# An attention and SwiGLU kernel: transposing x with VectorE and sixteen transfers instead of TensorE

## The chip, the core and the metric

The kernel runs on one core of one Trainium2 chip. The core has five engines that run their own instruction queues, each in order: TensorE (PE, matrix products into PSUM), VectorE (DVE), ScalarE (ACT), GpSimd (POOL) and SyncE (SP), which here only issues transfers. Transfers are carried by 16 DMA engines. The metric is the device time of one execution in microseconds, the median of several executions. A profiled execution, whose trace is read in this document, has its own span, which is a little shorter than the timed number.

## The reference

Two operations in sequence, all in float32:

```python
kv  = einsum('bhsd,bhse->bhde', k, v)          # per batch and head, 64 x 64
out = einsum('bhsd,bhde->bhse', q, kv)
x   = out / sqrt(mean(out*out, -1) + 1e-6) * g_norm
x   = x.transpose(0, 2, 1, 3).reshape(4608, 512)
y   = (silu(x @ w_gate) * (x @ w_val)) @ w_out  # 512 -> 1536 -> 512
```

There are 8 batches, 8 heads, 576 positions and head dimension 64, so x has 8 x 576 = 4608 rows of 8 x 64 = 512 columns. The root mean square is taken over each head's 64 values, so it is done per row and head. The weights arrive as 64-bit words and are rounded to float32 in the kernel.

## The kernel before, in words

**Blocks.** The 4608 rows are cut into nine blocks of 512 rows (four tiles of 128). One block holds rows of one or two batches. For every block the kernel has an *up stage* (x times w_gate and w_val, silu, product: h of 1536 x 512) and a *down stage* (h times w_out). Attention for block n+1 is worked in between: k^T v during the up stage of block n, q k^T v, the norm and the transposition during the down stage of block n. The class `Att` holds attention, `Ffn` the two stages.

**Matrix products.** They are done by a Strassen-Winograd scheme: seven products (numbered 1 to 7) of half-sized operands instead of eight, with sums of operands made beforehand on VectorE and GpSimd and sums of results made on VectorE. From block 2 on (`DEEP = 2`), the up stage does this at two levels (class `Inner`); the operand sums on the weight side were put into DRAM once and are streamed back as tiles `t` (L698). The sums on the x side are made by `sums` (L378): four of the first level in the tile `x`, which has seven parts of which 0 to 3 are x itself, then four of the second level, partly in the tile `xi`. The up stage's products are at L617. The down stage (class `Down`, products at L468) is one level deep; its products come in the order 1, 5, 6, 7, 2, 4, 3, here called P1, P5 and so on. Each is 24 matmuls of 128x128 by 128x256, as the profile counts them. P1, P6, P7 and P4 add onto one PSUM tile from the pool b and ScalarE copies out its state in between; P2 uses a; P5 and P3 use c. P5, P7 and P4 need operand differences `t` made by GpSimd (`turn_t`, L753).

**Attention in the down stage.** `steps` (L421) gives three pieces of work that `down` (L881) places behind P1, P6 and P2:

- behind P1, the first half (two of four row tiles): `product` (L312; q k^T v, 64 matmuls of 64x64, results in one PSUM tile of pool m and one of a; squares on ScalarE; sums of squares on VectorE, L338), `root` (L340; 1/sqrt by an integer first guess and three Newton steps on VectorE, 11 small instructions), `scale` (L358; x times the root, from PSUM into the tile `xts`);
- behind P6, `turn_x(0)` (L365): TensorE transposes the first half, eight 128x128 blocks through an identity matrix into PSUM pool m (L373), ScalarE copies them out with the gain g_norm (L374); then the second half of attention, its results in pools m and b;
- behind P2, `turn_x(1)`, then `sums`.

x has to be transposed because TensorE contracts over partitions: attention leaves rows on partitions, the up stage needs columns there.

**q, transposed already otherwise.** From block 3 on (`TURNED = 3`) q is not transposed by TensorE: `load_quarters` (L235) loads it in pieces of 32 columns, so that each 32x32 block lands where its transpose belongs, and VectorE transposes every 32x32 block in place of its own (L300). These are 32 transfers, or 16 for the last block, with rows of 128 bytes (L247); `down` issues them behind P5 for the block after the next.

**What sets the order.** The code emits instructions in the order that the loops give; the tile framework then orders every engine's queue by its own estimate of when things are ready, and sets semaphores for the dependencies between engines. Since a queue runs in order, an instruction that waits also holds what stands behind it on its engine. Tiles come from pools with a fixed number of buffers (`ring()`, five buffers of 128x2048, holds q transposed, the squares, `xts`, and the result sums; x has one buffer; PSUM pools a, b, c, m have 1, 3, 2 and 2 banks), and a new tile waits until the old one in its buffer is no longer read. Transfers also wait for the earlier one on the same of eight completion semaphores.

Of the kernel before, what the change touches and what calls it, by code (L numbers as in the profile page):

```python
# [8 lines left out]
F32 = mybir.dt.float32  # L9
# [3 lines left out]
ACT = mybir.ActivationFunctionType  # L13

P = 128
# [3 lines left out]
def kernel(  # L19
# [41 lines left out]
    nc = tc.nc  # L61
# [6 lines left out]
    HB = BLK // 2  # L68
    HD = DM // 2
    NB = NT // BLK  # L70
# [9 lines left out]
    def pool(name, bufs, **kw):  # L80
        return ctx.enter_context(tc.tile_pool(name=name, bufs=bufs, **kw))
# [4 lines left out]
    x_pool = pool("x", 1)  # L86
# [7 lines left out]
    a_psum = pool("a_psum", 1, space=PS)  # L94
    b_psum = pool("b_psum", 3, space=PS)
    c_psum = pool("c_psum", 2, space=PS)
    m_psum = pool("m_psum", 2, space=PS)
# [4 lines left out]
    gain = consts.tile([P, 1], F32, name="gain")  # L102
# [12 lines left out]
    def ring():  # L115

        return r_pool.tile([P, 4, BLK], F32, name="r")
# [67 lines left out]
    class Att:  # L185
# [126 lines left out]
        def product(self, i, pools=None):  # L312

            pools = pools or (m_psum, m_psum)
            self.ps[i] = [pool.tile([P, 2, NS, D], F32, name=pool.name[0]) for pool in pools]
            for t in range(2):  # L320
                for j in range(NS):
                    for b, _, p0, p1 in self.parts(2 * i + t):
                        for p in range(p0, p1, D):
                            for u in range(2):
                                rows = slice(u * D, (u + 1) * D)
                                nc.tensor.matmul(  # L326
                                    self.ps[i][u][p : p + D, t, j, :],
                                    lhsT=self.qt[rows, 2 * i + t, j, p : p + D], rhs=kvs[b % 3][rows, j, :],
                                    start=True, stop=True,
                                )  # L330
            if self.z is None or self.n:
                self.z = st_pool.tile([P, 2, 2, 2, NS], F32, name="z")
            if i == 0:
                self.sq = ring().rearrange("p f (t j d) -> p f t j d", t=2, j=NS)
            for u in range(2):
                sq = self.sq[:, 2 * i + u]
                nc.scalar.activation(out=sq, in_=self.ps[i][u], func=ACT.Square)  # L337
                nc.vector.tensor_reduce(out=self.z[:, i, u], in_=sq, axis=mybir.AxisListType.X, op=OP.add)  # L338
# [26 lines left out]
        def turn_x(self, i):  # L365
            if i == 0:
                self.x = x_pool.tile([P, 7, 2, HB], F32, name="x")
            xt = self.xts[:, i].rearrange("p t j u d -> p t j (u d)")
            for j in range(0, NS, 2):
                ps = m_psum.tile([P, 2, 2, P], F32, name="m")  # L370
                for e in range(2):
                    for t in range(2):
                        nc.tensor.transpose(ps[:, e, t], xt[:, t, j + e], ident)  # L373
                nc.scalar.activation(  # L374
                    out=self.x[:, 2 * i + j // 2], in_=ps.rearrange("p e t c -> p e (t c)"), func=ACT.Copy, scale=gain
                )

        def sums(self):  # L378

# [41 lines left out]
        def steps(self):  # L421


            def last():
                self.turn_x(1)
                if self.n:
                    self.sums()

            def middle():
                self.turn_x(0)  # L430
                self.half(1, (m_psum, b_psum))


            return [lambda: self.half(0, (m_psum, a_psum)), middle, last]

    CHAIN = {1: ("b", True), 6: ("b", False), 7: ("b", False), 4: ("b", False), 2: ("a", True),
             5: ("c", True), 3: ("c", False)}
# [5 lines left out]
    DEEP = 2  # L443

    TURNED = 3

    class Quad:


        def __init__(self, steps):  # L450
            self.steps = steps
            self.ps, self.room = {}, None

            self.apart = {}
# [94 lines left out]
    class Inner:  # L549
# [36 lines left out]
        def whole(self, g, o):  # L586

            return self.shared[g][:, o].rearrange("p f e q t -> p (f e) (q t)")
# [242 lines left out]
    class Ffn:  # L831
# [49 lines left out]
        def down(self, nxt):  # L881

            down = self.down_
            fill = dict(zip((1, 6, 2), nxt.steps() if nxt else ()))
            for p in (1, 5, 6, 7, 2, 4, 3):
                if p == 1:
                    down.turn_t(7, self.ended)
                if p == 6:
                    down.turn_t(4, nxt.halves[0] if nxt and nxt.n >= TURNED else None)
                down.multiply(p)  # L890
                self.make(12)
                if p == 5:
                    for i in range(2):
                        self.loads(i)
                if p in fill:
                    fill[p]()
                if p == 1:
                    down.turn_s3()
# [45 lines left out]
    blocks = [Att(n) for n in range(NB)]  # L944
# [8 lines left out]
    for n in range(NB):  # L953
        ffn = Ffn(n, blocks[n])
        nxt = blocks[n + 1] if n + 1 < NB else None
# [38 lines left out]
            nxt.turn()  # L994
        if n + 2 < NB:
            blocks[n + 2].load_kv(0)
        ffn.loads = blocks[n + 2].load_q if TURNED - 2 <= n < NB - 2 else lambda i: None
        ffn.down(nxt)
        if n == 0:

# [34 lines left out]
```

## Time and profile before

| | before |
|---|---|
| timed, median of 3 (us) | 1053.01 (1052.91 to 1053.46) |
| span of the profiled execution (us) | 1051.5 |
| TensorE matmul busy | 1026.1 us, 98% |
| VectorE busy | 706.9 us, 67% |
| GpSimd busy | 368.7 us, 35% |
| ScalarE busy | 232.7 us, 22% |
| L373, TensorE transposes of x | x144, 19.6 us |
| L374, ScalarE copies of them with the gain | x36, 22.9 us |
| L300, VectorE transposes of q in 32x32 blocks | x12, 14.7 us |
| L247, transfers of q with 128-byte rows | x176, 8 to 64 KB each |

How to read a row of the profile: a source line, an engine, an operation, the tiles it writes and reads, the shapes, how often, the busy time and the mean duration, and the engine's idle time just before with what ended it. In a timeline the first two numbers are the start and the length in microseconds; equal neighbours are merged and counted. Matmuls overlap one another, so their pitch, from start to start, is what they cost and not their duration. Source lines of element-wise helpers are those of the helper (L111 to L113: add, subtract, multiply), so such rows are told apart by their tiles. SPq rows are transfers being issued on SyncE's queue. Nine blocks follow each other; from block 3 to block 7 the pattern repeats every 109.98 us in the trace.

### The profile page before, as it was taken

To read this page: it belongs to the slowest core of one execution; us is meant where nothing else is said; L and a number is where in the kernel's file an instruction comes from. 1 tells how busy PE (TensorE), PEld (TensorE's weight loads), DVE (VectorE), ACT (ScalarE), POOL (GpSimd) and SP (SyncE) were. 2 spreads that over 40 slices of the span, in tenths; PEclk is the share of its full clock that TensorE was granted. 3 is DMA by queue.
4 is the path that set the end of the run, shared out by engine and by line. 5 is a ranking of instruction groups with operands and counts; after the bars stand their busy time and mean duration, and the time that the engine had idled before them with its cause. 6 is when DMAs were issued, how large, how long until landed. Compare 5 with 4: busy or idle time off the path is not lost.

```text
span 1051.5 us, 21628 instructions
## 1 busy us (share of the span) xinstructions
PE 1026.1 (98%) x8684; PEld 923.0 (88%) x8684; DVE 706.9 (67%) x1257; ACT 232.7 (22%) x368; POOL 368.7 (35%) x280
## 2 busy tenths in 40 slices
PE   5899999999999999999999999999999999999998
PEld 4644688778899989998999899989999899989997
DVE  2999696888556856575666666676668566855661
ACT  2666211211212121212111211221111211122110
POOL 0000443435025612463146305640455036512670
PEclk9899999999999999999999999999999999999999
DMA  9787304775467536763576347634773266126611
GB/s 247 209 265 245 106 1 125 183 208 130 127 197 245 111 87 188 230 153 79 162 240 177 91 127 228 213 71 130 218 208 68 92 204 191 51 81 203 193 31 41
DMA packets 204356, 161.87 MB, mean 154 GB/s; under 512 B 73952, under 2 KB 179552, under 8 KB 204256
## 3 DMA queue, kind: packets, MB, share of 16 engines
q1 hardware_dynamic: 204192, 160.48, 52.6%
q8 instruction: 69, 1.13, 0.5%
q14 instruction: 31, 0.25, 0.1%
q0 software_dynamic: 64, 0.00, 0.0%
HBM read 138.02 MB, written 22.41 MB: 153 GB/s over the span
## 4 chain that ended last, share of the span: by engine, by line
PE 91%; DVE 4%; DMA 2%; SPq 2%; issue 1%; ACT 0%; POOL 0%; DVEq 0%; ACTq 0%; POOLq 0%
PE b L617 25%; PE b L468 20%; PE c L617 12%; PE c L468 10%; PE a L617 6%; PE a L468 5%; PE c L911 4%; PE b L911 4%; PE m L285 2%; PE m L373 1%; PE m L326 1%; SPq L228 1%; PE b L326 1%; DMA ld<-in_moe_w_gate_dram 1%; DVE xi L112 1%
## 5 line engine op out<-in xcount | busy, mean ns | idle before, releaser
L111 POOL TENSOR_TENSOR r<-r 128x256 f32<-128x256 f32 (+1 forms) x105 | 110.1, 1055 | 326.9 <-DVE r L111 276.2
L111 DVE TENSOR_TENSOR r<-b,r 128x512 f32<-128x512 f32 (+1 forms) x273 | 161.9, 606 | 61.8 <-PE b L617 57.2
L112 POOL TENSOR_TENSOR t<-wo 128x512 f32<-128x512 f32 x81 | 115.7, 1452 | 187.1 <-DVE wo L111 109.3
L111 DVE TENSOR_TENSOR r<-c,r 128x512 f32<-128x512 f32 (+1 forms) x179 | 108.7, 617 | 96.5 <-PE c L617 53.6
L617 PE MATMUL b<-x,t 128*128 128x128 f32 x1092 | 150.7, 275 | 0.0
L617 PEld LDWEIGHTS b<-x,t 128*128 128x128 f32 x1092 | 136.5, 192 | 0.4
L111 DVE TENSOR_TENSOR r<-a,r 128x512 f32<-128x512 f32 (+1 forms) x99 | 62.5, 631 | 80.9 <-PE a L617 50.9
L113 POOL TENSOR_TENSOR h<-r 128x1024 f32<-128x1024 f32 (+1 forms) x40 | 81.6, 2054 | 90.7 <-DVE r L111 76.9
L617 PE MATMUL c<-xi,t 128*128 128x128 f32 x840 | 112.2, 275 | 0.0
L617 PEld LDWEIGHTS c<-xi,t 128*128 128x128 f32 x840 | 102.8, 192 | 0.0
L468 PE MATMUL b<-wo,h 128*128 128x256 f32 x432 | 98.8, 381 | 0.1
L468 PE MATMUL b<-t,h 128*128 128x256 f32 x432 | 97.1, 382 | 0.0
L468 PEld LDWEIGHTS b<-wo,h 128*128 128x128 f32 x432 | 80.6, 190 | 12.5 <-DVE h L113 2.5
L468 PEld LDWEIGHTS b<-t,h 128*128 128x128 f32 x432 | 80.8, 190 | 10.9 <-issue 0.2
L631 ACT COPY r<-b 128x512 f32<-128x512 f32 x63 | 36.9, 585 | 218.2 <-PE b L617 191.0
L617 PE MATMUL b<-xi,t 128*128 128x128 f32 x588 | 79.8, 276 | 0.0
L617 PEld LDWEIGHTS b<-xi,t 128*128 128x128 f32 x588 | 72.4, 192 | 0.0
L617 PE MATMUL b<-x,wg 128*128 128x128 f32 x336 | 52.7, 279 | 0.0
L617 PE MATMUL b<-x,wv 128*128 128x128 f32 x336 | 51.3, 275 | 0.0
L468 PE MATMUL c<-t,s 128*128 128x256 f32 x216 | 48.9, 383 | 0.0
L338 DVE TENSOR_REDUCE z<-r 128x8 f32<-128x512 f32 x36 | 23.0, 678 | 37.9 <-ACT r L337 37.8
L468 PE MATMUL a<-wo,h 128*128 128x256 f32 x216 | 48.3, 379 | 0.0
(129 smaller groups left out, 1641.2 us busy)
## 6 DMA issues: line engine op xcount, KB each, us to landing
t<-w SPq DMA_DIRECT2D x336, 256.0 KB, 3.1
out_dram<-r SPq DMA_DIRECT2D x17, 512.0 KB, 3.0
ld<-in_moe_w_gate_dram SPq DMA_DIRECT2D x12, 512.0 KB, 4.9
ld<-in_moe_w_val_dram SPq DMA_DIRECT2D x12, 512.0 KB, 5.7
ld<-in_moe_w_out_dram SPq DMA_DIRECT2D x12, 512.0 KB, 4.4
w<-t SPq DMA_DIRECT2D x18, 256.0 KB, 2.3
w<-xi SPq DMA_DIRECT2D x12, 384.0 KB, 3.0
ld<-in_k_dram SPq DMA_DIRECT2D x26, 160.0 KB, 3.2
```

What stands on the lines that cost most here:

```text
L111: add = lambda e, o, a, b: e.tensor_tensor(out=o, in0=a, in1=b, op=OP.add)
L112: sub = lambda e, o, a, b: e.tensor_tensor(out=o, in0=a, in1=b, op=OP.subtract)
L113: mul = lambda e, o, a, b: e.tensor_tensor(out=o, in0=a, in1=b, op=OP.mult)
L228: nc.sync.dma_start(out=t, in_=src[self.n, 2 * j : 2 * j + 2, s0 : s0 + m * D].rearrange("h (p t) d -> p h (t d)", t=m),)
L285: nc.tensor.matmul(self.kv_ps[r][u * D : (u + 1) * D, j, :], lhsT=self.k[j, r][:, u, c, :], rhs=self.v[j, r][:, u, c, :], start=(c == 0), ...
L326: nc.tensor.matmul(self.ps[i][u][p : p + D, t, j, :], lhsT=self.qt[rows, 2 * i + t, j, p : p + D], rhs=kvs[b % 3][rows, j, :], start=True, ...
L338: nc.vector.tensor_reduce(out=self.z[:, i, u], in_=sq, axis=mybir.AxisListType.X, op=OP.add)
L373: nc.tensor.transpose(ps[:, e, t], xt[:, t, j + e], ident)
L468: nc.tensor.matmul(banks[e][:, e], lhsT=lhsT, rhs=rhs, start=first and i == 0 and (e == 0 or banks[0] is not banks[1]), stop=i == self.ste ...
L617: nc.tensor.matmul(ps[:, i, f], lhsT=self.weight(o, p, f), rhs=self.operand(o, p), start=first and (i, f) == (0, 0), stop=True, skip_group ...
L631: nc.scalar.copy(out=dst, in_=ps)
L911: nc.tensor.matmul(t, lhsT=w[f // 2][:, i, P * (f % 2) : P * (f % 2 + 1)], rhs=x[:, i, of], start=(i == 0), stop=(i == NS - 1),)
```

## The change

From block 3 on (six of the nine blocks, made in the down stages of blocks 2 to 7), attention in the down stage is placed differently, and x is transposed without TensorE:

- behind P1 stands `whole`: both halves of q k^T v, one `root` over both, both scalings, and `blocks_x`, two VectorE transposes that turn every 32x32 block of `xts` into the buffer that held the squares;
- `place_x`, behind P5 in the code, puts the blocks where they belong in the tile `x`: 16 transfers from SBUF to SBUF, each of 32 partitions by 16 pieces of 32 values (64 KB in 128-byte rows), eight issued by SyncE and eight by ScalarE;
- behind P2 stand `gain_x`, two ScalarE operations of 128x1024 in place with the gain, and `sums`;
- in these stages P6 comes ahead of P5;
- from block 2's down stage on, the q loads for the block after the next are emitted ahead of the down stage instead of behind P5;
- from block 3 on, one tile `z` for the sums of squares serves both halves.

Blocks 0 to 2 keep the old way.

```diff
@@ -328,7 +328,7 @@
                                     lhsT=self.qt[rows, 2 * i + t, j, p : p + D], rhs=kvs[b % 3][rows, j, :],
                                     start=True, stop=True,
                                 )
-            if self.z is None or self.n:
+            if self.z is None or 0 < self.n < TURNED:
                 self.z = st_pool.tile([P, 2, 2, 2, NS], F32, name="z")
             if i == 0:
                 self.sq = ring().rearrange("p f (t j d) -> p f t j d", t=2, j=NS)
@@ -375,6 +375,32 @@
                     out=self.x[:, 2 * i + j // 2], in_=ps.rearrange("p e t c -> p e (t c)"), func=ACT.Copy, scale=gain
                 )
 
+        def blocks_x(self):
+
+
+            turned = self.sq.rearrange("p f t j d -> p (f t j d)").rearrange("p (i x) -> p i x", i=2)
+            for i in range(2):
+                nc.vector.transpose(
+                    out=turned[:, i].rearrange("p (j t c) -> p t j c", t=2, c=P),
+                    in_=self.xts[:, i].rearrange("p t j u d -> p t j (u d)"),
+                )
+            self.turned = turned
+
+        def place_x(self):
+            src = self.turned.rearrange("p i (x c) -> p (i x) c", c=P)
+            self.x = x_pool.tile([P, 7, 2, HB], F32, name="x")
+            dst = self.x[:, 0:4].rearrange("p o k (t c) -> p (o k t) c", c=P)
+            rows = [slice(32 * r, 32 * (r + 1)) for r in range(4)]
+            for a in range(4):
+                for b in range(4):
+                    queue = nc.scalar if b % 2 else nc.sync
+                    queue.dma_start(out=dst[rows[b], :, rows[a]], in_=src[rows[a], :, rows[b]])
+
+        def gain_x(self):
+            for i in range(2):
+                x = self.x[:, 2 * i : 2 * i + 2].rearrange("p o k t -> p (o k t)")
+                nc.scalar.activation(out=x, in_=x, func=ACT.Copy, scale=gain)
+
         def sums(self):
 
             a11, a12, a21, _, s1, s3, s4 = (self.x[:, i] for i in range(7))
@@ -421,6 +447,22 @@
         def steps(self):
 
 
+            def whole():
+                self.product(0, (m_psum, a_psum))
+                self.product(1, (m_psum, b_psum))
+                self.root(0, 2)
+                for i in range(2):
+                    self.scale(i)
+                self.halves.append(self.scaled)
+                self.blocks_x()
+
+            def end():
+                self.gain_x()
+                self.sums()
+
+            if self.n >= TURNED:
+                return {1: whole, 5: self.place_x, 2: end}
+
             def last():
                 self.turn_x(1)
                 if self.n:
@@ -431,7 +473,7 @@
                 self.half(1, (m_psum, b_psum))
 
 
-            return [lambda: self.half(0, (m_psum, a_psum)), middle, last]
+            return {1: lambda: self.half(0, (m_psum, a_psum)), 6: middle, 2: last}
 
     CHAIN = {1: ("b", True), 6: ("b", False), 7: ("b", False), 4: ("b", False), 2: ("a", True),
              5: ("c", True), 3: ("c", False)}
@@ -881,15 +923,15 @@
         def down(self, nxt):
 
             down = self.down_
-            fill = dict(zip((1, 6, 2), nxt.steps() if nxt else ()))
-            for p in (1, 5, 6, 7, 2, 4, 3):
+            fill = nxt.steps() if nxt else {}
+            for p in (1, 6, 5, 7, 2, 4, 3) if 5 in fill else (1, 5, 6, 7, 2, 4, 3):
                 if p == 1:
                     down.turn_t(7, self.ended)
                 if p == 6:
                     down.turn_t(4, nxt.halves[0] if nxt and nxt.n >= TURNED else None)
                 down.multiply(p)
                 self.make(12)
-                if p == 5:
+                if p == 5 and self.n == DEEP - 1:
                     for i in range(2):
                         self.loads(i)
                 if p in fill:
@@ -994,7 +1036,11 @@
             nxt.turn()
         if n + 2 < NB:
             blocks[n + 2].load_kv(0)
-        ffn.loads = blocks[n + 2].load_q if TURNED - 2 <= n < NB - 2 else lambda i: None
+        if TURNED - 2 <= n < NB - 2:
+            ffn.loads = blocks[n + 2].load_q
+            if n >= DEEP:
+                for i in range(2):
+                    ffn.loads(i)
         ffn.down(nxt)
         if n == 0:
 
```

## The prediction

> **What bounds the kernel now.** I read the page's busy table, then the waits of the matmul engine, then one down stage instruction by instruction (block 3's, in which the attention of block 4 is made; a block repeats every 109.98 us, so it stands for the others), and last the transfers with 128-byte rows.
>
> ```profile
> PE 1026.1 (98%) x8684; PEld 923.0 (88%) x8684; DVE 706.9 (67%) x1257; ACT 232.7 (22%) x368; POOL 368.7 (35%) x280
> ```
>
> TensorE is the bound, and more strictly than 98% says: asked for waits from 460 us on, the matmul engine has none, and a whole block period (362.89 to 472.87 us) has 109.96 us busy in 109.98. So a TensorE instruction taken out shortens the span by its pitch, and a delay elsewhere costs nothing until a matmul starts late. TensorE's rows of the stage:
>
> ```profile
> 479.24 5.34 PE L468 MATMUL b<-wo,h 128*128 128x256 f32 x24
> 484.42 1.04 PE L373 MATMUL m<-ident,r 128*128 128x128 f32 x8
> 486.93 5.45 PE L468 MATMUL b<-t,h 128*128 128x256 f32 x24
> 492.21 5.34 PE L468 MATMUL a<-wo,h 128*128 128x256 f32 x24
> 497.39 1.04 PE L373 MATMUL m<-ident,r 128*128 128x128 f32 x8
> 498.27 5.35 PE L468 MATMUL b<-t,h 128*128 128x256 f32 x24
> 503.45 5.34 PE L468 MATMUL c<-wo,h 128*128 128x256 f32 x24
> 508.63 0.61 PE L617 MATMUL b<-x,wg 128*128 128x128 f32 x4
> ```
>
> Take starts, not durations (matmuls overlap): a product P is 5.18 us, 5.28 after a q k^T v half. The two transpose groups hold TensorE for 485.39 - 484.42 = 0.97 and 498.27 - 497.39 = 0.87 us. The second half takes 486.93 - 485.39 = 1.54 us where the first took 473.96 - 472.87 = 1.09: its m matmuls start at 485.85, just after ScalarE emptied the first transpose bank at 485.80.
>
> What must come out in time for the row at 508.63 is x and its sums on VectorE:
>
> ```profile
> 497.60 0.69 DVE L111 TENSOR_TENSOR r<-a,r 128x512 f32<-128x512 f32 x1 [3.87 <-PE a L468]
> 498.20 1.75 DVE L112 TENSOR_TENSOR h<-h 128x1536 f32<-128x1536 f32 x1
> 499.87 0.69 DVE L111 TENSOR_TENSOR x<-x 128x512 f32<-128x512 f32 x1
> 500.47 2.14 DVE L112 TENSOR_TENSOR x<-x 128x512 f32<-128x512 f32 x3
> 504.77 1.09 DVE L112 TENSOR_TENSOR x<-xi,x 128x896 f32<-128x896 f32 x1
> ```
>
> The sums start behind the work that follows P2 and finish x at 505.86, 2.8 us ahead of the up stage. The nearest rows for the new transfers are q's:
>
> ```profile
> 788.92 5.24 SPq L247 DMA_DIRECT2D ld<-in_q_dram  x10
> ...
> q1 hardware_dynamic: 8670, 1.05, 36.3%
> ```
>
> Those ten move 64 KB each in 128-byte rows, the new transfers' shape: 0.53 us apart on one queue, landing about 3 us after issue. The second line is a window of 18 us (463 to 481) with 1.05 MB of such rows: 0.363 x 18 = 6.5 us of all 16 DMA engines per MB.
>
> **What the skill says.** "VectorE: DVE Perf Modes", "The three transpose paths": VectorE transposes 32x32 blocks only, so the blocks still have to be placed. The trace has 1.23 us for 128x1024 (L300), and that price is used. "DMA: Bandwidth & Descriptors", "Issuing engines are not separate DMA queues": two issuing engines share the 16 DMA engines and save only issue time; only SP issues in volume here, so no run yet shows the saving. The same page, "Why small descriptors are slow (HBM only)": transfers from SBUF to SBUF do not suffer from short rows; no row shows it, and I price them as q's. "SBUF — State Buffer", "Who interferes with whom": a tensor_scalar in a 2-port mode and GpSimd block each other. The trace agrees: L344 and L347 take 1.17 and 1.19 us while GpSimd's L112 runs, 0.17 each in the second half.
>
> **The change, part by part**, for six down stages (n = 2 to 7, making blocks 3 to 8). T is the start of q k^T v: 472.87 in the stage shown.
>
> 1. Removed on TensorE: 16 transposes, 0.97 + 0.87 = 1.84 us, and the wait in the second half, 0.45 us, since no transpose bank is left to be emptied; one stage also has one 5.28 product less, 0.10. Together 2.39 us a stage, and 6 x 2.39 = 14.3 us if nothing is given back. The new TensorE times: both halves to T+2.2, P6 to 7.5, P5 12.6, P7 17.8, P2 23.0, P4 28.2, P3 33.4, where the up stage starts (35.8 before).
> 2. P6 ahead of P5: P6 adds onto the bank of P1, which ScalarE copies out at T+0.2 to 0.8, under the halves. P5's t tiles come free 5.2 us later. No cost.
> 3. VectorE, nearly the same work earlier: four reductions to T+5.1; the first root operation waits for GpSimd's L112 (busy to T+6.1), one root instead of two (11 instructions at about 0.2) to 8.2, four scalings at about 0.65 to 10.8, two transposes at 1.23 to 13.3. GpSimd's t of P4 now starts at 10.8 instead of 9.4; P4 needs it at 23. Hidden behind P6 to P7.
> 4. The 16 transfers, eight on SP and eight on ScalarE, from T+13.3. Low end: both queues at a pitch of 0.53, four each until the eight completion semaphores have to come back (3 us), four more, landing 3 us later: about 8 us, above the 6.5 us of the engines. High end: the queues gain nothing from being two, 16 x 0.53 + 3 = 11.5. I take 8.5: landed at T+21.8. On ScalarE the copy after P7 (done at 17.8, needed by P4 at 23.0) stands behind the eight issues, which end by T+18.5, or 22 at the high end: hidden. SP's first t loads of the next block stand behind them too: they moved from T+7.4 to about T+18.5, for use at T+33.
> 5. The gain: two in-place 128x1024 operations, 1.06 each by row L644, instead of four of 0.69. T+21.8 to 23.9. VectorE comes to the sums only at T+26.2: after P2 (23.2) 0.69 + 1.75, and now the addition after P7 (0.69) too. Sums as before 6.0 us, x finished at T+32.2. Its first reader of the last quarter is P6 of the up stage, 0.9 us after T+33.4. So landing may slip from 21.8 to about 25.8 before TensorE waits: a 12.5 us phase.
> 6. q loads for block n+2 ahead of P1: SP issued them at T-9.7 to T+7.2 already, since they wait only for their buffers; done before T+13.3. Nothing. The two z tiles become one: nothing.
> 7. What is not alike in the six: the built order of the changed program. In stage n = 4 the addition after P3 stands ahead of the last x sum on VectorE: it ends at T+34.2, the sum at 35.4, while TensorE has only 14 matmuls of 0.11 to do until 34.9: about 0.6 us lost. In stage n = 5 the gain stands behind the copy after P4 on ScalarE (T+29.0), so it ends at 31.1; on VectorE the addition after P3 and three additions of the up stage stand between the sums: the second-level sum that P5 of the up stage needs ends at 38.1, finished x at 41.0, the last sum at 42.5. TensorE's own work, with some q k^T v matmuls of the next block pulled ahead, reaches to 35, 36.1, 39.3 and 41.9: waits of about 0.6 + 2.1 + 1.8 + 0.6 = 5 us. Bounds: 2 us (if most of the additions overlap) to 7.
>
> Sum: 14.3 - 0.6 - 5.0 = 8.7 us. Of the profiled 1051.5 that leaves 1042.8; the timed median lies 1.5 above that span (1053.01), so **1044.3**.
>
> **Rivals.**
> - *Nothing given back*: stages 4 and 5 absorb their order too. For: before, the sums had 2.8 us of slack. Against: the order on an engine's queue is fixed. 1053.0 - 14.3 = 1038.7.
> - *Transfers late in part*: the phase takes 13 to 14 us. Then four to five stages wait one to two microseconds each, and 5 to 9 us go back: 1047 to 1053. For: SBUF to SBUF and ScalarE's queue are unseen, and a single q issue once took 1.71 us. Against: even one queue would need 11.5.
> - *Slower*: one mechanism, the placement at T+13.3. Five stages (the sixth waits for P4 anyway) lose what exceeds 12.5 us. At 14.3 us the 8.7 are gone; above 14.7 the kernel is slower than 1055.1. A phase of 16 us gives 1053.0 - 8.7 + 5 x (16 - 12.5) = about 1062. For: a pitch of 0.9 instead of 0.53 on queues that serialize would do it. Against: the measured pitch.
> - *The change moves nothing on TensorE* is excluded: its order shows no transposes in these stages.
>
> **How the numbers follow.** Likeliest case 0.56 (own range 1041.5 to 1047), nothing given back 0.17, transfers late in part 0.17 (of which 0.05 ends within 0.2%), slower 0.10. Within 0.2% is about what a measurement of this kernel cannot tell from no change. So faster 0.56 + 0.17 + 0.12 = 0.85, same 0.05, slower 0.10. The range of 1038 to 1051.5 takes in the first two cases and most of the third.
>
> **What would show it.** Right: no transposes in six stages; P7 directly behind P5; second half near 1.1 us; placement of 8 to 9 us from about T+13.3; no TensorE wait at up starts of blocks 3, 4, 7 and 8, under 1 us at block 5, about 5 at block 6. Wrong: landing later than T+26; TensorE waits at every up start; issues on ScalarE far above 0.5 us; or a copy on ScalarE, stuck behind its issues, that holds P4.

## The result, and the profile after

The changed kernel takes 1042.79 us (1041.99 to 1043.23, four runs), the kernel before 1053.24 in the same comparison: a ratio of 0.9898 as recorded (the quotient of the two medians is 0.9901), 95% interval 0.9881 to 0.9915. The forecast was 1044.3, faster. The profiled span fell from 1051.5 to 1040.8 us.

Stage n stands here for the down stage of block n, in which x of block n+1 is made. The engine line of the page, and the matmul engine's timeline from P6 on in stage 3, where T, the start of q k^T v, is 471.01 (472.87 before; start and length in us):

```profile
PE 1015.1 (98%) x8588; PEld 911.7 (88%) x8588; DVE 702.9 (68%) x1203; ACT 230.9 (22%) x356; POOL 369.3 (35%) x280
...
473.04 5.45 PE L510 MATMUL b<-wo,h 128*128 128x256 f32 x24
478.32 5.34 PE L510 MATMUL c<-t,s 128*128 128x256 f32 x24
...
488.68 5.34 PE L510 MATMUL a<-wo,h 128*128 128x256 f32 x24
493.96 0.79 PE L285 MATMUL m<-ld 64*64 64x64 f32 x34
494.68 5.45 PE L510 MATMUL b<-t,h 128*128 128x256 f32 x24
499.96 5.34 PE L510 MATMUL c<-wo,h 128*128 128x256 f32 x24
505.14 0.61 PE L659 MATMUL b<-x,wg 128*128 128x128 f32 x4
```

TensorE has 96 instructions fewer (16 in each of six stages), and L373 is gone here. Both halves of q k^T v last 473.04 - 471.01 = 2.03 us. One row was not expected: k^T v of the block after the next (L285) stands between P2 and P4. The up stage starts at T+34.13. What has to be ready for it comes over VectorE, the two issuing queues and ScalarE; here VectorE, then ScalarE, then SyncE in the same stage:

```profile
481.86 2.36 DVE L383 STREAM_TRANSPOSE r<-r 128x1024 f32<-128x1024 f32 x2
...
496.94 0.68 DVE L111 TENSOR_TENSOR x<-x 128x512 f32<-128x512 f32 x1
...
501.84 1.09 DVE L112 TENSOR_TENSOR x<-xi,x 128x896 f32<-128x896 f32 x1
```

```profile
484.30 6.30 ACTq L397 DMA_DIRECT2D x<-r  x8
490.64 0.58 ACT L850 COPY r<-b 128x512 f32<-128x512 f32 x1 [11.54 <-DMA x<-r]
494.13 2.19 ACT L402 ACTIVATE x<-x,gain 128x1024 f32<-128x1024 f32 x2 [2.91 <-DMA x<-r]
```

```profile
484.29 7.38 SPq L397 DMA_DIRECT2D x<-r  x8
```

The transposes end at T+13.2, both queues issue from T+13.3, ScalarE's eight issues are done at T+19.6 and SyncE's at T+20.7, the last transfer lands at T+22.81, the gain runs from T+23.1 to 25.3, the sums from T+25.9, and x is finished at T+31.9. The copy after P7 (L850) waits behind the issues and ends at T+20.2; P4, which needs its bank, could start at T+22.95, behind P2.

Stage by stage, from one T to the next (the last to the end of the span), in us:

| down stage n | 2 | 3 | 4 | 5 | 6 | 7 |
|---|---|---|---|---|---|---|
| before | 109.98 | 109.98 | 109.98 | 109.98 | 107.08 | 141.58 |
| after | 107.88 | 107.88 | 107.82 | 110.52 | 104.53 | 139.04 |
| saved | 2.10 | 2.10 | 2.16 | -0.54 | 2.55 | 2.54 |

The sum is 10.9 us. Five stages save 2.1 to 2.55; stage 5, where x of block 6 is made, gives back 0.54. So three questions go to experiments: what the 2.1 to 2.55 consist of, where the rest went, and how much room the sixteen transfers have.

### The profile page after: what moved, and what is told of

It is laid out like the page before. It is cut to its first block, busy times and chain, and to the rows that moved or that the text cites. A ratio compares the mean times of both kernels' runs of the same rounds, so it can differ in the third digit from the quotient of the medians.

```text
span 1040.8 us, 21533 instructions
## 1 busy us (share of the span) xinstructions
PE 1015.1 (98%) x8588; PEld 911.7 (88%) x8588; DVE 702.9 (68%) x1203; ACT 230.9 (22%) x356; POOL 369.3 (35%) x280
## 4 chain that ended last, share of the span: by engine, by line
PE 91%; DVE 4%; DMA 2%; SPq 1%; issue 1%; POOL 0%; ACT 0%; DVEq 0%; POOLq 0%; ACTq 0%
PE b L659 25%; PE b L510 20%; PE c L659 12%; PE c L510 9%; PE a L659 6%; PE a L510 5%; PE b L953 4%; PE c L953 4%; PE m L285 2%; PE m L326 1%; SPq L228 1%; DVE xi L112 1%; DMA w<-t 1%; PE m L373 1%; DMA ld<-in_moe_w_gate_dram 1%
## 5 line engine op out<-in xcount | busy, mean ns | idle before, releaser
L510 PEld LDWEIGHTS b<-wo,h 128*128 128x128 f32 x432 | 80.0, 190 | 12.6 <-DVE h L113 2.5
L659 PE MATMUL b<-xi,t 128*128 128x128 f32 x588 | 79.7, 276 | 0.0
L510 PE MATMUL c<-wo,h 128*128 128x256 f32 x216 | 48.1, 379 | 0.0
```

The source lines that it names most:

```text
L510: nc.tensor.matmul(banks[e][:, e], lhsT=lhsT, rhs=rhs, start=first and i == 0 and (e == 0 or banks[0] is not banks[1]), stop=i == self.ste ...
L659: nc.tensor.matmul(ps[:, i, f], lhsT=self.weight(o, p, f), rhs=self.operand(o, p), start=first and (i, f) == (0, 0), stop=True, skip_group ...
```

## The experiments

The first kernel takes the transfers out again. The others keep the change and add to it, fix the order of some instructions, or put one part of it another way (all transfers on one queue, P5 ahead of P6). Every ratio is to the kernel before in the same comparison.

### Without the transfers: where the saving comes from

The halves stay together and P6 ahead of P5, but x is transposed by TensorE again, behind P5 and P2:

```diff
                 self.halves.append(self.scaled)
-                self.blocks_x()
...
-                self.gain_x()
+                self.turn_x(1)
                 self.sums()
...
-                return {1: whole, 5: self.place_x, 2: end}
+                return {1: whole, 5: lambda: self.turn_x(0), 2: end}
```

> The changed kernel with x transposed by TensorE again: both halves of q k^T v stay together behind P1 and P6 stays ahead of P5, but the 32x32 transposes, the sixteen transfers and the separate gain are gone; eight TensorE transposes stand behind P5 and eight behind P2. Theory A (the gain is the TensorE time of the transposes; the rest of the change gives only the 0.45 us wait of the second half): saves 6 x 0.45 to 6 x 0.55 of 1053.2, so about 1050 us. Theory B (the gain comes from putting the halves together and from the order, the transposes were hidden): close to the changed kernel, 1043 us.

Measured: 1049.31 us (1048.76 to 1049.86), ratio 0.9958 [0.9944, 0.9972]; stages of 109.18 us, 109.33 in one. So 0.80 us a stage come from putting the halves together and from the order of the products, somewhat more than expected. The two transpose groups in stage 3 of this kernel (T = 473.13):

```profile
485.62 1.04 PE L373 MATMUL m<-ident,r 128*128 128x128 f32 x8
486.50 5.35 PE L509 MATMUL b<-t,h 128*128 128x256 f32 x24
...
496.86 1.04 PE L373 MATMUL m<-ident,r 128*128 128x128 f32 x8
497.73 5.35 PE L509 MATMUL b<-t,h 128*128 128x256 f32 x24
```

Both halves take 2.03 us against 1.09 + 1.54 before, which is 0.60; the first group now stands between two products and takes 0.88 instead of 0.97 us, which is 0.09; and one product less takes 5.28 instead of 5.18, which is 0.10. That is the 0.80, up to rounding. The TensorE transposes themselves cost 0.88 + 0.87 = 1.75 us, and the same 1.75 is the difference to the stages without them, below: 109.18 - 107.43.

### The order on two queues: what stage 5 lost

In stage 5 (T = 686.71) the profile after shows this on SyncE, ScalarE and TensorE:

```profile
692.74 10.52 SPq L247 DMA_DIRECT2D ld<-in_q_dram  x5
703.37 6.63 SPq L397 DMA_DIRECT2D x<-r  x8
```

```profile
715.86 0.58 ACT L854 COPY r<-b 128x512 f32<-128x512 f32 x1 [9.41 <-PE b L510]
716.34 2.19 ACT L402 ACTIVATE x<-x,gain 128x1024 f32<-128x1024 f32 x2
```

```profile
722.27 0.44 PE L285 MATMUL m<-ld 64*64 64x64 f32 x8
723.31 0.71 PE L659 MATMUL a<-x,t 128*128 128x128 f32 x4 [0.60 <-DMA t<-w]
723.95 0.34 PE L285 MATMUL m<-ld 64*64 64x64 f32 x8
...
727.17 2.05 PE L659 MATMUL c<-xi,t 128*128 128x128 f32 x16 [0.29 <-DVE xi L111]
```

SyncE begins the eight transfers at T+16.7 instead of T+13.3, and the last lands at T+25.0. The gain stands behind the copy after P4 (L854) on ScalarE, TensorE waits, and k^T v lies in pieces between the up stage's matmuls. The edit puts the copy after P4 behind the gain, and the addition after P3 behind the last sum for x, by an order between instructions of one queue:

```diff
-            nc.scalar.copy(out=self.o2[:, :, 0:HD], in_=self.ps["b"])
+            copied = nc.scalar.copy(out=self.o2[:, :, 0:HD], in_=self.ps["b"])
+            if self.nxt and self.nxt.n >= TURNED:
+                behind(copied, self.nxt.gained)
...
-            self.add_c(self.o1[:, :, HD:DM], self.u2)
+            added = self.add_c(self.o1[:, :, HD:DM], self.u2)
+            if self.nxt and self.nxt.n >= TURNED:
+                behind(added, self.nxt.summed)
```

> The changed kernel, with the queue order of the fourth changed stage (block 5's down stage) made like the others': ScalarE's copy after P4 is put behind the gain, VectorE's addition after P3 behind the sums. Theory A (in that stage the fixed order of the queues makes the matmuls at the start of block 6 wait): the stage takes about 2.7 us less, so 1042.8 becomes about 1040.1 us, and no matmul pitch above 0.45 us is left at the start of block 6. Theory B (that stage is late because its transfers or the next block's weight tiles come late): no change, 1042.8 us, and the waits stay.

Measured: 1041.47 us (1040.76 to 1041.89), ratio 0.9883 [0.9868, 0.9898]. The waits that the profile listed for the matmul engine in that stage (0.60, 0.29 and 0.19 us) are gone, but stage 5 fell only from 110.52 to 109.35, less than half of what theory A said. So these two orders were worth 1.17 us, and more than half of what that stage lost was no wait that the profile lists.

### k^T v out of the down stage

```diff
             def third():
-                nxt.kv(0)
+                if n >= TURNED:
+                    with tc.issue_after(before_.mm.ins):
+                        nxt.kv(0)
+                else:
+                    nxt.kv(0)
```

Here `before_.mm` is the latest matmul of the down stage, so k^T v may not be pulled ahead of it.

> The changed kernel, with the k^T v matmuls of the block after next kept out of the down stage (17 groups of them had moved between P2 and P4 in four stages). Theory A (leaving and re-entering the run of large matmuls costs about 0.45 us a stage, and nothing was idle there to be filled): 3 x 0.45 to 4 x 0.45 us less, so 1042.8 becomes about 1041.2 us. Theory B (they fill time in which TensorE would wait for x): no change or slower, 1042.8 to 1045 us.

Measured: 1040.89 us (1040.64 to 1042.35), ratio 0.9881 [0.9866, 0.9896]. Stages 2, 3 and 4 take 107.43, 107.43 and 107.38: 0.45 us less each, as expected. In the timeline of this kernel P4 follows P2 and the up stage P3 with nothing between:

```profile
494.57 5.34 PE L510 MATMUL b<-t,h 128*128 128x256 f32 x24
499.75 5.34 PE L510 MATMUL c<-wo,h 128*128 128x256 f32 x24
504.93 0.61 PE L659 MATMUL b<-x,wg 128*128 128x128 f32 x4
```

The same matmuls are still worked, in the up stage. Summed from start to start, the 64x64 matmuls of k^T v take 2.76 us a stage in the changed kernel, where they lie in runs of 34, 38 and 72, and 2.51 us here, in two runs of 72; the seven down products take 36.95 us there and 36.75 here. So the third run, between P2 and P4, costs 0.45 us: 0.25 on itself and 0.20 on the products around it. Both edits together:

> The two order fixes together. Theory A (TensorE never has to wait for x, and all of the removed time is kept): all six stages save 2.55 us as the last two did in the changed kernel, 15.3 us of 1053.2, so about 1038 us. Theory B (one bound replaced by another: when the orders are mended the start of the up stage waits for x by itself): 1040 us or more, with waits at the up starts.

Measured: 1040.97 us (1040.28 to 1041.86), ratio 0.9879 [0.9865, 0.9894]; stage 5 109.80. Theory A was wrong by 2.4 us there; the time is rival B's, but the waits at the up starts that B asked for are not there. No wait of a matmul is listed, but k^T v, held back to the end of the down stage alone, now lies in five pieces between the first matmuls of the up stage. The next kernel holds it behind the latest up matmul (`ffn.mm` in place of `before_.mm`), which places it alike in all stages. Called "three orders fixed" from here:

> The changed kernel with three orders fixed and nothing else: on ScalarE the copy after P4 stands behind the gain, on VectorE the addition after P3 stands behind the last sum for x, and the k^T v matmuls of the block after the next stand behind the latest matmul of the up stage, so that none of them lies among the down products or between single up matmuls. Theory A (all six stages save the same 2.55 us against the kernel before, and what blocks 5 and 6 lost was the order of the queues and the scattered k^T v matmuls): six stages of 107.43, 107.43, 107.43, 107.43, 104.53 and 139.03 us, a span of about 1037.7 and a time of about 1038.5 to 1039.5. Rival B (block 6's up stage is late because x itself is late there, whatever the order): its stage stays at about 109.8, and the span at 1040.0.

Measured: 1040.11 us (1039.90 to 1040.75), ratio 0.9873 [0.9859, 0.9886]; stage 5 109.35. Five stages came as theory A said, and the span, 1038.4 us, is nearer to its 1037.7 than to rival B's 1040.0. Stage 5 is nearer to rival B's 109.8: the pieces are gone, and nothing is won by that against the first two orders alone (109.35 us both times). VectorE in that stage (T = 685.49) names what is left:

```profile
714.03 1.42 DVE L112 TENSOR_TENSOR x<-x 128x512 f32<-128x512 f32 x2
720.75 0.69 DVE L111 TENSOR_TENSOR r<-a,r 128x512 f32<-128x512 f32 x1 [5.31 <-PE a L665]
721.36 1.08 DVE L111 TENSOR_TENSOR xi<-x 128x896 f32<-128x896 f32 x1
```

The second-level sums for block 6 stand between additions of the up stage, from T+35.9 on, though their operands are there at T+30.0. The tile framework, which makes this order, is called the planner from here. A fourth order, the up stage's first additions behind the last sum:

```diff
-                add(nc.vector, dst, ps, dst)
+                self.sums_first(add(nc.vector, dst, ps, dst))
...
+        def sums_first(self, added):
+            if self.ffn.n >= TURNED and self.d == 0 and self.g < 2:
+                behind(added, self.ffn.att.summed)
```

> The kernel with the three orders fixed, and a fourth: on VectorE the first additions of the up stage stand behind the last second-level sum for x. In the kernel with three orders fixed this differs in the making of block 6 alone, where the second-level sums run from T+35.9 to T+41.2 between additions of the up stage, though the first-level sums end at T+30.0. Theory A (that order is what the stage loses): the sums run from T+30.0 to T+34.3, against T+33.0 in the other stages, so the stage loses at most 1.3 us of the 1.9 it lost: 107.4 to 108.7 us instead of 109.35, and a time 0.7 to 1.9 us lower, 1038.2 to 1039.4. Rival B (the late landing at T+24.8 is what it loses, and the order only follows it): the stage stays at about 109.3 us, 1040.

Measured: 1038.68 us (1038.37 to 1039.53), ratio 0.9852 [0.9836, 0.9869], the lowest median of all runs (the intervals of two later kernels overlap with its own). Stage 5 takes 107.38 like the others, though the last transfer of that stage still lands at T+24.7. The sums in stage 5 (T = 685.88), without a gap:

```profile
713.01 0.69 DVE L111 TENSOR_TENSOR x<-x 128x512 f32<-128x512 f32 x1 [1.12 <-ACT x L402]
...
719.05 1.09 DVE L112 TENSOR_TENSOR xi<-x 128x896 f32<-128x896 f32 x1
```

They end at T+34.3, 1.0 us after the up stage's start, and no wait of a matmul is listed. So all 3.1 us that stage 5 lost (2.55 + 0.54) came from the order of the queues: with the data as late as before, the loss is gone.

### One issuing queue instead of two

```diff
-                    queue = nc.scalar if b % 2 else nc.sync
+                    queue = nc.sync
```

On the kernel with three orders fixed:

> As the kernel with the three orders fixed, but all sixteen transfers are issued by SyncE. Theory A (two issuing queues shorten the phase; a queue alone issues one such transfer every 0.53 to 0.65 us): the phase from the first issue to the last landing is 16 x 0.53 + 3 = 11.5 to 16 x 0.65 + 3 = 13.4 us instead of 9.5 to 10.2, and lands at T+24.8 to T+26.7. With 12.5 us of slack that costs TensorE between 0 and 0.9 us a stage, at most 5 us in all: a time of 1038.5 to 1044. Rival B (two queues gain nothing, since both share the 16 DMA engines and the eight semaphores): the phase stays at 9.5 to 10 us and the time is that of two queues. Rival C (one queue serializes with the landings): over 15 us and 1050 or more.

Measured: 1050.91 us (1049.99 to 1051.48), ratio 0.9974 [0.9964, 0.9984]: 11 us given back, far above theory A's number, though the phase is what it said. The number is rival C's, but its phase of over 15 us is not there. In stage 3 (T = 473.01) SyncE issues one transfer every 0.675 us, and the last lands at T+25.5, 12.25 us after the first issue (up to 13.8 in other stages). VectorE there:

```profile
501.06 0.69 DVE L111 TENSOR_TENSOR x<-x 128x512 f32<-128x512 f32 x1 [2.65 <-DMA t<-w]
501.67 2.14 DVE L112 TENSOR_TENSOR x<-x 128x512 f32<-128x512 f32 x3
508.37 0.69 DVE L111 TENSOR_TENSOR r<-a,r 128x512 f32<-128x512 f32 x1 [4.57 <-ACT r L679]
508.98 1.08 DVE L111 TENSOR_TENSOR xi<-x 128x896 f32<-128x896 f32 x1
```

The first-level sums end at T+30.8; then VectorE stands still for 4.57 us, because an addition of the up stage was put ahead of the second-level sums. It is the order that stage 5 had before, now in all six stages: stages 2 and 3 take 109.45 us, 2.02 more than with two queues, and stage 5, which had lost it already, hardly more than before. Whether the slack of theory A was there all the same, the next run tells, with the fourth order added:

> All sixteen transfers on SyncE, as before, but the first additions of the up stage stand behind the last second-level sum. The landing should stay at T+25.5, the gain at T+28.0, first-level sums at T+30.8, and the second-level sums then end at T+35.1 instead of T+41.2. Theory A (the landing is within the slack, and the order that the planner made for a later landing is what cost 2.02 us in each stage): 107.4 to 108.0 us a stage, a time of 1038.5 to 1042.5. Rival B (the landing is beyond the slack, whatever the order): TensorE waits at the start of the up stage and a stage takes 108.5 to 109.5 us, 1045 to 1051.

Measured: 1039.53 us (1038.86 to 1039.70), ratio 0.9858 [0.9843, 0.9872]. The issues on SyncE in stage 3 (T = 471.45), and VectorE:

```profile
484.72 10.75 SPq L397 DMA_DIRECT2D x<-r  x16
```

```profile
499.49 0.69 DVE L111 TENSOR_TENSOR x<-x 128x512 f32<-128x512 f32 x1 [2.63 <-ACT x L402]
...
505.52 1.09 DVE L112 TENSOR_TENSOR xi<-x 128x896 f32<-128x896 f32 x1
506.53 0.68 DVE L111 TENSOR_TENSOR r<-c,r 128x512 f32<-128x512 f32 x1
```

The last sum ends at T+35.2, two microseconds after the up stage has started, with no wait of a matmul listed and stages of 107.38. So the landing was within the slack, and the order was the loss. That order is TensorE's too: the planner puts the first up product that reads `xi` 2.7 us behind the start of the up stage in this kernel, against 0.9 in the changed one, so the slack shown is that of both orders together. In stage 5 of this run the last transfer lands at T+27.2, 13.9 us after the first issue, without a wait too.

### More transfers: where the room ends

Each of the sixteen is followed on its queue by one more transfer of 16 KB (or by three), into parts of x that the sums overwrite later:

```diff
                     queue.dma_start(out=dst[rows[b], :, rows[a]], in_=src[rows[a], :, rows[b]])
+                    for c in range(1):
+                        queue.dma_start(out=dup[rows[b], 4 * c : 4 * c + 4, rows[a]], in_=src[rows[a], 4 * c : 4 * c + 4, rows[b]])
```

> As the kernel with the three orders fixed, but each of the sixteen transfers is followed on its queue by another of 16 KB in 128-byte rows, which is additional work: it writes a part of x that the sums overwrite later. 32 transfers in all. Theory A (the placement has a slack of about 12.5 us, and what exceeds it is lost once in each stage): by eights of 3 to 4.5 us, 32 transfers take about 13.5 to 16 us, so each of five or six stages loses 1 to 3.5 us: a time of 1044 to 1059. Rival B (the slack is much larger, since the first up products need only early parts of x): no more than 1 us lost in all, 1038.5 to 1040. Rival C (the issues on ScalarE hold its copy after P7, and with it P4): TensorE waits ahead of P4 and not at the start of the up stage.

Measured: 1058.50 us (1056.34 to 1058.84), ratio 1.0043 [1.0031, 1.0056]. The size is theory A's, the place rival C's. The waits of the matmul engine after block 2 (total, times, longest), then ScalarE's copy after P7 in stage 3 (T = 472.86), and the P4 that waits for it with the P3 behind it:

```profile
PE b L519 <- ACT r L859: 11.5, 6, 2.3
PE b L668 <- DVE x L112: 1.0, 1, 1.0
```

```profile
497.42 0.59 ACT L859 COPY r<-b 128x512 f32<-128x512 f32 x1 [16.47 <-DMA x<-r]
```

```profile
498.15 7.02 PE L519 MATMUL b<-t,h 128*128 128x256 f32 x24 [2.28 <-ACT r L859]
505.01 5.34 PE L519 MATMUL c<-wo,h 128*128 128x256 f32 x24
```

ScalarE is through with its sixteen issues only at T+24.5, and the copy behind them holds P4, not the start of the up stage.

The waits are 12.5 us, but the kernel is 18.4 us slower than the one with three orders fixed. Most of the rest is TensorE's clock. Around the end of three of the six waits ahead of P4 (2.28, 2.22 and 2.00 us) the clock granted to TensorE was half of the full one for 3.41 us, and P4 took 6.86 to 6.94 us up to the next start; after the other three (1.40, 1.44 and 2.18 us) the clock stayed full, and P4 took 5.25 to 5.26. That makes 4.9 us. With three more transfers each (`range(3)`):

> As the kernel with 32 transfers, but each of the sixteen is followed by three of 16 KB: 64 transfers in all. Theory A (what exceeds 12.5 us is lost once in each stage): a phase of about 22 to 28 us, so 9.5 to 15.5 us lost in each of six stages, 57 to 93 us in all: 1095 to 1130, slower than the kernel before. The stages must be longer by the same amount as the phase is, one for one. Rival B (part is absorbed by k^T v and other matmuls that can be pulled ahead): less than one for one, 1060 to 1090.

Measured: 1124.22 us (1123.83 to 1125.66), ratio 1.0674 [1.0658, 1.0691]: stages 2 to 5 take 120.8 to 121.6 us, and the same copy makes 70.2 us of waits in six stages. Within theory A's range, but again in front of P4. The clock shows on the page of this run, where each digit is the clock in a fortieth of the span, in tenths of full speed, and 9 is 90% or more:

```profile
PEclk9899999999999989997999899998999799979999
```

At the end of each of the six waits (11.1 to 12.7 us) it was half, and P4 took 6.75 to 8.06 us, 14.0 us in all above 5.25 each. 70.2 + 14.0 = 84.2 us, and the kernel is 84.1 us slower than the one with three orders fixed.

### P5 ahead of P6, as before

```diff
-            for p in (1, 6, 5, 7, 2, 4, 3) if 5 in fill else (1, 5, 6, 7, 2, 4, 3):
+            for p in (1, 5, 6, 7, 2, 4, 3):
```

On the kernel with three orders fixed:

> The kernel with the three orders fixed, but with P5 ahead of P6 as it was before the change. Theory A (the place of P6 costs and brings nothing): the same stages within 0.1 us and the same time within 1 us, 1039 to 1041. Rival B (P5 first leaves the state of P1 in its bank longer, or makes the planner scatter up matmuls between P4 and P3, where four of them now stand): 0.3 to 1 us lost in each stage, 1042 to 1046.

Measured: 1066.33 us (1066.14 to 1067.64), ratio 1.0116 [1.0100, 1.0131]. Both theories are wrong by a wide margin: 26 us more than with P6 first, and slower than the kernel before. The waits of the matmul engine, then ScalarE and TensorE in stage 3 (T = 476.31):

```profile
PE b L516 <- ACT r L536: 16.3, 6, 3.4
```

```profile
489.60 6.33 ACTq L397 DMA_DIRECT2D x<-r  x8
495.97 0.58 ACT L536 COPY r<-b 128x512 f32<-128x512 f32 x1 [16.39 <-DMA x<-r]
```

```profile
483.61 5.34 PE L516 MATMUL b<-wo,h 128*128 128x256 f32 x24
488.79 5.34 PE L516 MATMUL a<-wo,h 128*128 128x256 f32 x24
496.70 5.42 PE L516 MATMUL b<-t,h 128*128 128x256 f32 x24 [2.56 <-ACT r L536]
```

The rows are P6, P2, which the planner put ahead here, and P7. With P5 first, P6 ends at T+12.6. That is 0.7 us before the transfers can start, and still the copy of its state (L536) stands behind ScalarE's eight issues in the queue, so P7, which adds onto that bank, waits until T+20.4. In the changed kernel that copy is done at T+8.1, ahead of the issues, and only the copy after P7 stands behind them, with 2.7 us to spare in stage 3.

Of the 26 us, 17.1 are waits: 16.3 for this copy, and one of 0.8 for the copy after P7. Another 7.9 are the clock again: around the end of four of the six waits for L536 (3.04, 1.98, 3.24 and 3.44 us) it was half for 3.4 us, or 6.8 after the last, and P7 took 6.81 to 8.20 us instead of 5.25; after those of 2.56 and 2.04 us it stayed full. The last 1.2 us were not taken apart. To see whether it is the issues on ScalarE, the same order with all transfers on SyncE and the four orders fixed:

> All sixteen transfers on SyncE, the four orders fixed, and P5 ahead of P6. With eight of the transfers on ScalarE, P5 first cost 26 us: the copy after P6 stood behind the eight issues on ScalarE, and P7 waited 2.4 to 3.8 us for it in every stage (L536, 16.3 us in all). Theory A (P6 ahead of P5 matters only because ScalarE issues transfers): with no issue on ScalarE the copy after P6 comes at once, no TensorE wait ahead of P7, stages within 0.3 us of those with P6 first (107.38), a time of 1038.5 to 1041.5. Rival B (P5 first costs by itself, by another bank or by up matmuls scattered among the last down products): P7 or P4 waits again, 1 to 4 us a stage, 1045 to 1064.

Measured: 1039.26 us (1038.95 to 1039.62), ratio 0.9865 [0.9849, 0.9882]; stages of 107.52. ScalarE's copy after P6 now comes at once, at T+12.7 (T = 470.64):

```profile
483.33 0.59 ACT L536 COPY r<-b 128x512 f32<-128x512 f32 x1 [9.41 <-PE b L516]
```

Without issues on ScalarE the place of P6 is worth 0.14 us a stage (107.52 against 107.38). With them it decides. Two things differ from the run before, the queue of the transfers and the fourth order; that order binds VectorE alone, and the wait in the run before was for a copy behind ScalarE's issues, but P5 first with two queues and four orders was not run.

## Why the prediction was right, step by step

The mechanism held: TensorE is the bound, what leaves it shortens the span, and the transfers come in time. The span fell by 10.7 us where the sum said 8.7. Errors of both signs met: the halves gave 1.0 us more than said, the orders in stages 4 and 5 cost 2.5 us less, and k^T v, which the sum left out, cost 1.35. So that the total came within 2 us is in part luck.

1. *Removed on TensorE, 2.39 us a stage.* It is 2.55 where nothing is lost. The difference is the halves: 2.03 us, not 2.2. The sizes of the parts held too: 0.80 for halves and order (0.55 predicted), 1.75 for the transposes (1.84 predicted).
2. *P6 ahead of P5: no cost.* True of the cost, and blind to the use. Without it the fast placement is a slow one: the step asked what the move harms, and not what would stand behind ScalarE's issues if P6 stayed. This was tried only with the three orders fixed, not in the changed kernel itself.
3. *VectorE's transposes end at T+13.3*: 13.2.
4. *The transfers: 8.5 us, between 8 and 11.5.* 9.5 us in stage 3 and 9.5 to 11.7 in the six, landing at T+22.8 in stage 3 instead of 21.8. The mean pitch there was 0.92 us on SyncE and 0.78 on ScalarE (0.71 to 1.01 over the stages), not q's 0.53. ScalarE's issues ended at T+19.6, not 18.5; the copy after P7 stayed hidden, by 2.7 us. Issues on ScalarE far above 0.5 us were listed as a sign of being wrong; they came, and did no harm in this order of the products. The price taken from q's rows held for the engines: in a window of 9.8 us (484.2 to 494) ScalarE's queue had this line,

```profile
q10 hardware_dynamic: 4224, 0.52, 32.1%
```

   which is 0.321 x 9.8 / 0.52 = 6.0 us of 16 engines per MB, against q's 6.5. The prediction was right not to lean on the Trainium skill here: "DMA: Bandwidth & Descriptors", "Why small descriptors are slow (HBM only)", says that transfers from SBUF to SBUF don't suffer from short rows, and at 128 bytes they took about the time of q's rows from DRAM. In the kernel with one queue and four orders they took 6.4 us per MB (54.6% of 10.8 us for 0.92 MB), and loads in longer rows, mostly weight-side tiles from DRAM, took 3.2 (79.7% of 28 us for 6.98 MB). No run here moves x from SBUF to SBUF in long rows, so what the short rows cost by themselves is not shown; for the price used the measurement decides. What the same page says in "Issuing engines are not separate DMA queues", that a second issuing engine saves only issue time, agrees: 9.5 us on two queues against 12.2 on one, and no time of the kernel (1038.68 against 1039.53, intervals that overlap).
5. *Sums from T+26.2, x finished at T+32.2*: 25.9 and 31.9. *Slack for a phase of 12.5 us*: at least that; phases of 12.2 to 13.9 us cost no wait once the sums stood first. But the slack is only there if the order grants it: the same landing with the planner's own order cost 2.02 us a stage.
6. *q loads ahead: nothing.* Nothing by themselves, as far as the runs show: the kernel without the transfers has the moved loads and the single z too, and its 0.80 us a stage is accounted for without them. But one sat in the wrong place. In stage 5 SyncE's last q load (8 KB) was issued at T+16.2, 8 us after the one before it and 0.02 us after ScalarE's second transfer had landed, and the eight transfers stood behind it. With no transfer on ScalarE SyncE starts at T+13.3 in that stage too (699.49, T = 686.21). So a load can wait for a transfer on the other issuing engine. The tie is the completion semaphore: in the trace the load waits for number 111, which is the one that ScalarE's second transfer had been given. In stage 4 it is SyncE's first transfer itself that shares number 113 with ScalarE's first, and it starts at T+15.7, 0.07 us after that one had landed.
7. *Stage 4 loses 0.6, stage 5 loses 5.* This is the step that failed in size. Stage 4 lost nothing by its order. Stage 5 lost 3.1 instead of 5. The first two orders gave back 1.17 of it; k^T v held back as well gave nothing more there (109.35 us both times); the last 1.97 came with the sums put ahead of the additions. That an order would cost there, and that ScalarE's copy after P4 and VectorE's additions were in it, was read rightly from the built order. The waits were not: the sum has 5.1 us of them, the profile lists 1.1, although x was finished at T+43.0 and not at 41.0. In the meantime TensorE worked up products in another order and matmuls of k^T v (L285), which the prediction calls q k^T v; how much of the difference each of these covered was not measured. Missed altogether was k^T v between P2 and P4, 0.45 us in stages 2 to 4 (in stage 5 it is part of the 3.1), though it stands in the same order: a run of small matmuls was taken as moved work that costs what it did before.

The sum with measured terms: 6 x 2.55 = 15.3, less 3 x 0.45 for k^T v and 3.1 for stage 5, is 10.85; the table's stages sum to 10.9. The span fell by 10.7, since the first of the six starts 0.25 us later (363.14, not 362.89; in the later runs, in which blocks 0 to 2 are worked in the same way, it lies anywhere from 363.1 to 364.5).

*The slower rival* put its break-even at a phase of 14.3 us, and a kernel slower by more than 0.2% above 14.7, by waits at the start of the up stage. With 32 transfers the kernel was slower by 0.4%, but this does not confirm the number: that kernel has three orders fixed, its phases were 13.9 to 19.9 us in the six stages, and 11.5 of its 12.5 us of waits are P4's for ScalarE's copy. Phases of up to 13.9 us, which by the rival cost something, cost nothing with the fourth order. The copy that holds P4 was listed under what would make the prediction wrong, not where the break-even was worked out.

## What to carry to other kernels

- When transfers are issued from a compute engine, count the issue time (here 0.8 us each with the waits) against the next thing that this engine owes the bottleneck, and order the bottleneck's work so that this debt is paid before the issues begin. Here the other order cost 26 us, and with the issues on SyncE and the fourth order it cost nothing that can be measured (1039.26 against 1039.53 us).
- A wait of TensorE can cost more than itself. After waits of about 2 us and more its clock was often half for a while, and the product behind the wait took 1.5 to 2.95 us longer. Look at the granted clock behind a wait before looking for another cause.
- A late transfer and a late order look alike in the waits. Ask when the operands were there: sums that stand behind additions although their inputs have been ready for 5 to 6 us need another order, not faster transfers. The planner made such an order by itself in six stages when the transfers moved to one queue.
- Read the built order for what is pulled into the bottleneck's gaps as well. The four orders fixed take the change from 1.0% to 1.5%.

## What was not expected of the hardware

- Thirty-four 64x64 matmuls between two products cost about 0.45 us a stage more than in the up stage, in three stages alike; one run of small matmuls more cost 0.25 us on these and 0.20 on the products.
- Around the end of the waits of TensorE in three runs the granted clock was half for 3.4 us or a multiple of it, in 13 of the 18 stages. No length of the wait decides it here: 1.98 us brought it on, 2.04, 2.18 and 2.56 did not, and those of 1.44 us and less did not either.
- Alone on SyncE a 64 KB transfer with 128-byte rows was issued every 0.675 us; on two queues at once the mean pitch of a stage was 0.71 to 1.01 on each. Two queues brought 16 landings from 12.2 to 9.5 us, not to half.
- A transfer on ScalarE's queue delayed a load on SyncE's by 8 us, because both had the same completion semaphore, and so the eight transfers behind it by 3.4 us.
